# Attention by query tile: heads inside, Q, K and V kept on chip in F32, bias rows made between the attention's instructions

## The chip, the cores and the metric

The kernel runs on one core of a Trainium2 chip. The metric is device time in microseconds, from one launch to its end; lower is better. Shown are the median of the runs and, for the profile, one execution taken by the hardware profiler.

## The reference

The program computes attention with a learned position bias, then a mixture of experts, then a gated feed-forward block. Only the attention is touched here:

```python
B, H, S, D = (2, 8, 576, 64)              # hidden 32
scores = scale * np.matmul(q, k.transpose(0, 1, 3, 2))
psi_rel = np.log1p(np.abs(rel))           # rel = i - j
psi_i = np.log1p(np.maximum(pos[:, None].astype(np.float32), 1.0))
x = (psi_rel / psi_i)[..., None]
h = np.maximum(x @ w1 + b1, 0.0)
bias = h @ w2                             # [S, S, H], the same for both batches
scores = scores + bias.transpose(2, 0, 1)[None, :, :, :]
scores = scores - np.max(scores, axis=-1, keepdims=True)
attn = np.exp(scores)
attn = attn / (np.sum(attn, axis=-1, keepdims=True) + 1e-09)
return np.matmul(attn, v).astype(np.float32)
```

The output, 1152 rows of 512, goes to an expert gate (8 logits a row, the largest decides), to the chosen expert, and to the last block.

## The kernel before

**Engines and order.** TensorE (PE) multiplies, VectorE (DVE), ScalarE (ACT) and GpSimd (POOL) work on tiles, SyncE (SP) issues the DMAs. The order on each engine is the order of the program text (`manual_schedule`); every engine takes its instructions strictly in turn and waits on semaphores.

**Bias phase** (`bias_phase`, lines 478 to 583). A group `m` covers 16 query rows. `relus` makes four ReLU tiles of 128 x 576 from a table of logarithms: three on DVE (line 539), one on ACT (line 542). Eight matmuls (line 547), in four column tiles of 32, multiply them by w2, which gives 16 rows for 8 heads. `evict` copies the 128 x 576 sum out of PSUM (ACT, line 554) and writes it to a table in DRAM (line 558). All 36 groups come before the attention. Between them the first head's Q and K are split.

**Loads** (`loader`, lines 226 to 260). For each head and batch a tile with Q and K twice over is read (line 241). It is split into a high part in F32R and the rest: by ACT and DVE for the first head, by POOL (lines 252 to 257) for the others, one head ahead.

**Attention** (`attn_phase`, lines 263 to 475). Heads are outside; within a head come nine units (batch, query tile of 128 rows; the fifth tile has 64 rows of each batch and is one unit). For unit `u` the program issues: the score of `u + 1` (line 304, four F32R matmuls of 288 columns, eight for the fifth tile); the exponential of `u - 1` on ACT with row sums (line 336); the bound of `u` on DVE (line 319: scores times -1/8 plus bias and the row minimum in one instruction; line 209 to 214 load the bias rows of a head from the table); four transposes of `u - 2` (line 344) and a copy of the 128 x 512 result by ACT or DVE (lines 350, 352); tail transposes (line 360, copied in lines 362, 364). In pieces between units: P·V for half a head (line 378, F32, V as four column tiles of 32, 256 or 320 query columns), its copy (line 384) and `folds` (line 397), which adds the gate weights to the output columns, divides by the row sums (lines 408 to 417), writes the head's columns of all rows to DRAM (line 419) and adds the gate logits up in `lg` (line 423).

**After it** `route` turns `lg` into lists of rows for each expert, and `moe` gathers the rows from DRAM and runs experts and feed-forward. Both begin with the last sum in `lg`.

The PSUM buffers of attention and bias share tags: "S" (scores and bias sums), "T" (transposes), "P" (P·V).

Of the kernel before, what the change touches and what calls it, by code (L numbers as in the profile page):

```python
# [20 lines left out]
NQ = 5  # L21
SK = 640
SQ = 640
# [31 lines left out]
LOADS = (0, 3)  # L55
SHARE = 0.7
ON_A = (0, 2, 4, 6)
CUTS = (1, 3)
# [12 lines left out]
ND = 3  # L71
# [36 lines left out]
def pack(inputs):  # L108
    q, k, v = inputs["q"], inputs["k"], inputs["v"]
    qk = np.zeros((B, H, 128, SQ + SK), np.float32)  # L110
    qt, kt = q.transpose(0, 1, 3, 2), k.transpose(0, 1, 3, 2)
    for r in (slice(0, 64), slice(64, 128)):
        qk[:, :, r, :512] = qt[..., :512]
        for b in range(B):
            qk[b, :, r, 512 + b * 64:576 + b * 64] = qt[b, :, :, 512:]
        qk[:, :, r, SQ:SQ + 64] = kt[..., 512:]
        qk[:, :, r, SQ + 64:] = kt
    vt = np.zeros((H, 128, B, 6, D), np.float32)
    for t in range(4):
        vt[:, :, :, t] = v[:, :, t * 128:(t + 1) * 128].transpose(1, 2, 0, 3)  # L120
    for r in range(2):
        vt[:, r * 64:r * 64 + 64, :, 4 + r] = v[:, :, 512:].transpose(1, 2, 0, 3)
# [4 lines left out]
    fold = np.zeros((128, H // 2, RW + E), np.float32)  # L127
    for r in range(2):
        fold[r * 64:r * 64 + 64, :, E:RW] = np.eye(D)[:, None]
        fold[r * 64:r * 64 + 64, :, :E] = wg[::2].transpose(1, 0, 2)  # L130
        fold[r * 64:r * 64 + 64, :, RW:] = wg[1::2].transpose(1, 0, 2)
    both = np.zeros((128, H, B, RW), np.float32)
    for h in range(H):
        for r in range(2):
            both[r * 64:r * 64 + 64, h, r] = fold[r * 64:r * 64 + 64, h // 2, h % 2 * E:h % 2 * E + RW]
    a = {
        "qk": qk,
        "v": vt,
        "both": both,
        "wb": np.tile(wb, (4, 1)),  # L140
        "fold": fold,
        "ew1": inputs["moe_w1"],
        "ew2": inputs["moe_w2"],

        "mwg": inputs["moe2_w_gate"].view(np.int64),
        "mwv": inputs["moe2_w_val"].view(np.int64),
        "mwo": inputs["moe2_w_out"].view(np.int64),
    }
    a.update(constants())
    return {n: np.ascontiguousarray(x) for n, x in a.items()}  # L150
# [8 lines left out]
def build(tc, ins, out, cap):  # L159
    nc = tc.nc  # L160
    cap = max(0, min(int(cap), N))
    with ExitStack() as ctx:
# [19 lines left out]
        with ExitStack() as pctx:  # L182
            ps = pctx.enter_context(tc.tile_pool(name="ps", bufs=2, space=PSUM))
            attention(tc, ins, cst, rt, lg, x_p, rows, out, ps)
# [3 lines left out]
def attention(tc, ins, cst, rt, lg, x_p, rows, out, ps):  # L188
    nc = tc.nc
    with ExitStack() as ctx:  # L190
# [6 lines left out]
        nc.vector.memset(zi, 0.0)
        b_p = ctx.enter_context(tc.tile_pool(name="ab", bufs=2))
        heads = {}

        def bias_of(h, t):

            if h not in heads:
                heads[h] = b_p.tile([128, NQ, S], F32, name="bias")
            to = heads[h][:, t]
            src = table[t].rearrange("(q h) j -> q h j", h=H)[:, h]
            if t == 4:
                for r in (slice(0, 64), slice(64, 128)):
                    nc.sync.dma_start(to[r], src)
            elif t % 2:  # L210
                nc.sync.dma_start(to[:, 64:], src[:, :512])
                nc.sync.dma_start(to[:, :64], src[:, 512:])
            else:
                nc.sync.dma_start(to, src)

        load, qk = loader(tc, ctx, ins), {}
        ctx.enter_context(tc.manual_schedule(engines=ENGINES))
        with ExitStack() as bctx:
            loads = bias_phase(tc, bctx, ins, cst, rt, table, bias_of, zi, ps, load, qk)
        nc.sync.dma_start(fold, ins["fold"])  # L220
        nc.sync.dma_start(both, ins["both"])
        with ExitStack() as actx:
            attn_phase(tc, actx, (load, qk, loads), cst, (heads, bias_of), (fold, both), lg, x_p, rows, zi, out, ps)


def loader(tc, ctx, ins):

    nc = tc.nc
    raw_p = ctx.enter_context(tc.tile_pool(name="araw", bufs=4))
    qk_p = ctx.enter_context(tc.tile_pool(name="aqk", bufs=4))  # L230
    v_p = ctx.enter_context(tc.tile_pool(name="av", bufs=3))
    V, A, P = nc.vector, nc.scalar, nc.gpsimd
    one = ctx.enter_context(tc.tile_pool(name="az", bufs=1))
    zero = one.tile([128, 1], F32, name="zero")
    V.memset(zero, 0.0)
    vs = {}

    def load(h, b, hi="P"):

        raw = raw_p.tile([128, SQ + SK], F32, name="raw")  # L240
        nc.sync.dma_start(raw, ins["qk"][b, h])
        if h not in vs:
            vs[h] = v_p.tile([128, B, 6, D], F32, name="vt")
            nc.sync.dma_start(vs[h], ins["v"][h])
        QK = qk_p.tile([128, SQ + SK], F32R, name="QK")
        K2 = qk_p.tile([128, SK], F32R, name="K2")
        yield QK[:, :SQ], QK[:, SQ:], K2, vs[h]
        for o, n in ((0, SQ), (SQ, SK)):
            if hi == "A":
                A.activation(QK[:, o:o + n], raw[:, o:o + n], AF.Copy)  # L250
            else:
                P.tensor_tensor(QK[:, o:o + n], raw[:, o:o + n], view(zero, 0, (0, n)), op=ALU.add)  # L252
            yield
        low = V if hi == "A" else P
        low.tensor_tensor(QK[64:, :SQ], raw[64:, :SQ], QK[64:, :SQ].bitcast(F32), op=ALU.subtract)
        yield
        low.tensor_tensor(K2, raw[:, SQ:], QK[:, SQ:].bitcast(F32), op=ALU.subtract)
        yield

    return load  # L260


def attn_phase(tc, ctx, load, cst, bias, fold, lg, x_p, rows, zi, out, ps):
    nc = tc.nc
    V, A = nc.vector, nc.scalar
    s_p = ctx.enter_context(tc.tile_pool(name="as", bufs=3))
    one = ctx.enter_context(tc.tile_pool(name="apt", bufs=1))
    fold, both = fold
    pts = [one.tile([128, 4, B, S], F32, name=f"pt{n}") for n in range(2)]
    tls = [one.tile([128, B, 320], F32, name=f"tl{n}") for n in range(2)]  # L270
    os = [one.tile([128, 512], F32, name=f"o{n}") for n in range(2)]
    o8s = [one.tile([128, 128], F32, name=f"o8{n}") for n in range(2)]
    for n in range(2):
        nc.gpsimd.memset(tls[n][64:, :, 256:], 0.0)
        nc.gpsimd.memset(o8s[n][:64, 64:], 0.0)
        nc.gpsimd.memset(o8s[n][64:, :64], 0.0)
    m_p = ctx.enter_context(tc.tile_pool(name="am", bufs=4))
    ident = cst[:, C_ID:C_ID + 128]
    load, qk, loads = load
    heads, bias_of = bias  # L280
    seq = []
    for h in range(H):
        seq += [(h, b, t) for b in range(B) for t in (0, 1)] + [(h, -1, 4)]
        seq += [(h, b, t) for b in range(B) for t in (2, 3)]
    mid = {}
    spare = ps.tile([128, 512], F32, name="tt", bufs=1)
    sco, ex, sums, xhs = {}, {}, {}, {}

    def batches(u):
        h, b, t = seq[u]  # L290
        return (b,) if t < 4 else (0, 1)

    def score(u):

        h, b, t = seq[u]
        sc = ps.tile([128, 2, 512], F32, name="sc", tag="S")
        lhs = []
        for bb in batches(u):
            Q, K1, K2, _ = qk[h, bb]
            lhs += [(Q[:, t * 128:(t + 1) * 128], K) for K in (K1, K2)]  # L300
        o = 0 if t % 2 else 64
        for c in range(2):
            for n, (l, K) in enumerate(lhs):
                nc.tensor.matmul(  # L304
                    sc[:, c, :288], l, K[:, o + c * 288:o + (c + 1) * 288], start=n == 0, stop=n == len(lhs) - 1
                )
        sco[u] = sc

    def bound(u):
        h, b, t = seq[u]  # L310
        sc = sco.pop(u)

        if t % 2 == 0:
            pair = s_p.tile([128, 2, S], F32, name="ex")
            ex[u], ex[u + 1] = pair[:, 0], pair[:, 1]
            mid[u] = pair.rearrange("p a b -> p (a b)")[:, 512:640]
        e = ex[u]
        mx = m_p.tile([128, 1], F32, name="mx")
        V.tensor_tensor_reduce(  # L319
            e.rearrange("p (c j) -> p c j", c=2),  # L320
            sc[:, :, :288],
            heads[h][:, t].rearrange("p (c j) -> p c j", c=2),
            scale=-0.125,
            scalar=3.0e38,
            op0=ALU.add,
            op1=ALU.min,
            accum_out=mx,
        )
# [1379 lines left out]
```

## Time and profile before

| | us |
|---|---|
| median of 3 runs | 458.8 |
| lowest, highest | 455.86, 459.73 |
| the profiled execution | 455.44 |
| its span, first to last instruction | 453.7 |
| DVE's first ReLU of the bias phase | 5.26 |
| first bound of the attention | 64.82 |
| last bound of the attention | 222.07 |
| last sum of the gate logits (0.23 long) | 233.33 |

The busy time of an engine counts the time in which at least one of its instructions was under way. For PE this includes the latency of a pipelined matmul, which its neighbours overlap. A matmul on F32 tiles appears as two instructions, one on F32R tiles as one. "Idle before" is the engine's wait just before an instruction, with what ended it. PEclk is the granted share of TensorE's full clock.

### The profile page before, as it was taken

The numbers are of one execution on the slowest core, as the hardware profiler recorded it, in microseconds if no ns is written. First come the engines' busy times: TensorE is split into PE (matmuls) and PEld (weight loads), VectorE is DVE, ScalarE is ACT, GpSimd is POOL, SyncE is SP. The second block draws the span as 40 slices with busy tenths as digits, with TensorE's granted clock in tenths as the row PEclk, the third lists the DMA queues.
The fourth block names the chain that finished last, engine by engine and source line by source line (L and its number), as shares of the span: only waits on it lengthen the run. The fifth ranks groups of instructions, "written<-read, shape, count | busy, mean of one in ns | idle before, by whom it ended". The sixth has DMA issues, their size and how long they took to land. (4 is left out here: it accounts for less than half of the span.)

```text
span 453.7 us, 9220 instructions
## 1 busy us (share of the span) xinstructions
PE 409.4 (90%) x3493; PEld 321.9 (71%) x3493; DVE 310.3 (68%) x653; ACT 236.3 (52%) x459; POOL 100.3 (22%) x89
## 2 busy tenths in 40 slices
PE   8999897998998899899848789999999999999993
PEld 5333356766766676666635789898799999999982
DVE  6999974556657566655557458785488888888441
ACT  5999876555555564546422238563335554433321
POOL 0500009827283837540003210000000000000012
PEclk9999998999999999999976589999999999999999
DMA  7557868827466373910147993859105644440002
GB/s 258 211 195 225 308 248 271 280 71 262 134 198 209 122 251 91 318 56 1 51 122 242 345 309 95 277 181 331 48 1 170 209 175 143 141 140 1 1 25 93
DMA packets 53766, 77.22 MB, mean 170 GB/s; under 512 B 15090, under 2 KB 34162, under 8 KB 53712
## 3 DMA queue, kind: packets, MB, share of 16 engines
q1 hardware_dynamic: 52912, 74.05, 49.5%
q0 software_dynamic: 800, 2.48, 1.6%
q8 instruction: 30, 0.49, 0.5%
q14 instruction: 24, 0.20, 0.1%
HBM read 59.95 MB, written 16.58 MB: 169 GB/s over the span
## 5 line engine op out<-in xcount | busy, mean ns | idle before, releaser
L319 DVE CUSTOM_DVE_ANT_0 ex<-sc,bias 128x576 f32<-128x576 f32 x72 | 53.5, 752 | 22.8 <-issue 10.5
L1133 PE MATMUL pg<-x2l,swh 128*128 128x256 f32 (+1 forms) x192 | 58.1, 302 | 0.0
L1133 PE MATMUL pg<-x2h,swh 128*128 128x256 f32 (+1 forms) x192 | 58.0, 302 | 0.0
L1133 PE MATMUL pg<-x2h,swl 128*128 128x256 f32 (+1 forms) x192 | 57.9, 302 | 0.0
L336 ACT ACTIVATE ex<-ex,mx 128x576 f32<-128x576 f32 x72 | 55.4, 770 | 4.0 <-DVE mx L319 2.8
L304 PE MATMUL sc<-QK 128*128 128x288 f32 x160 | 52.0, 342 | 6.0 <-DVE mx L319 5.7
L547 PE MATMUL pb<-r,w 128*32 128x288 f32 x576 | 54.8, 415 | 2.6 <-ACT e L554 1.0
L539 DVE TENSOR_SCALAR r<-ltab,slope,neg 128x576 f32<-128x576 f32 x108 | 53.5, 570 | 0.1
L352 DVE COPY pt<-tp 128x512 f32<-128x512 f32 x40 | 27.6, 690 | 31.9 <-PE tp L344 31.8
L547 PEld LDWEIGHTS pb<-r,w 128*32 128x32 f32 x576 | 21.6, 108 | 35.3 <-DVE r L539 13.4
L304 PE MATMUL sc<-K,QK 128*128 128x288 f32 x160 | 45.3, 299 | 0.0
L304 PEld LDWEIGHTS sc<-QK 128*128 128x128 f32 x160 | 30.5, 191 | 20.6 <-issue 10.8
L344 PE MATMUL tp<-cst,ex 128*128 128x128 f32 x288 | 43.9, 276 | 0.3 <-ACT ex L336 0.3
L252 POOL TENSOR_TENSOR QK<-raw,zero 128x640 fp32r<-128x640 f32 x28 | 34.5, 1253 | 33.4 <-DMA raw<-in_qk 18.6
L1140 ACT ACTIVATE wh<-wr 128x608 fp32r<-128x608 f32 (+2 forms) x13 | 8.8, 674 | 61.8 <-DVE wr L1136 61.8
L350 ACT ACTIVATE pt<-tp 128x512 f32<-128x512 f32 x32 | 19.1, 597 | 40.0 <-PE tp L344 39.1
L1158 POOL DMA_INDIRECT out<-xr,ids x2 | 2.0, 1012 | 170.7 <-DMA xr<-rows,ri 170.7
L1133 PEld LDWEIGHTS pg<-x2h,swh 128*128 128x128 f32 x192 | 36.2, 189 | 2.0 <-issue 0.8
L1133 PEld LDWEIGHTS pg<-x2l,swh 128*128 128x128 f32 x192 | 36.1, 188 | 0.9
L344 PEld LDWEIGHTS tp<-cst,ex 128*128 128x128 f32 x288 | 35.8, 142 | 1.2 <-ACT ex L336 0.8
L1133 PEld LDWEIGHTS pg<-x2h,swl 128*128 128x128 f32 x192 | 36.2, 188 | 0.0
L378 PE MATMUL po<-pt,vt 128*32 128x320 f32 (+1 forms) x512 | 35.8, 410 | 0.1
(191 smaller groups left out, 894.8 us busy)
## 6 DMA issues: line engine op xcount, KB each, us to landing
wr<-in_ew SPq DMA_DIRECT2D x24, 512.0 KB, 4.9
table<-e SPq DMA_DIRECT2D x36, 288.0 KB, 2.1
raw<-in_qk SPq DMA_DIRECT2D x16, 640.0 KB, 6.1
w<-in_mwg SPq DMA_DIRECT2D x12, 512.0 KB, 3.6
w<-in_mwv SPq DMA_DIRECT2D x12, 512.0 KB, 4.7
w<-in_mwo SPq DMA_DIRECT2D x12, 512.0 KB, 6.7
bias<-table SPq DMA_DIRECT2D x16, 288.0 KB, 6.3
bias<-table SPq DMA_DIRECT2D x16, 256.0 KB, 6.1
```

Of the source, the lines that this page charges most:

```text
L252: P.tensor_tensor(QK[:, o:o + n], raw[:, o:o + n], view(zero, 0, (0, n)), op=ALU.add)
L304: nc.tensor.matmul(sc[:, c, :288], l, K[:, o + c * 288:o + (c + 1) * 288], start=n == 0, stop=n == len(lhs) - 1)
L319: V.tensor_tensor_reduce(e.rearrange("p (c j) -> p c j", c=2), sc[:, :, :288], heads[h][:, t].rearrange("p (c j) -> p c j", c=2), scale=-0 ...
L336: A.activation(ex[u], ex[u], AF.Exp, bias=mx, scale=-1.0, accum_out=sums[h][:, col:col + 1])
L344: nc.tensor.transpose(x[:, kt], e[:, kt * 128:(kt + 1) * 128], ident)
L350: A.activation(to, x, AF.Copy)
L352: V.tensor_copy(to, x)
L378: nc.tensor.matmul(po[s * 32:s * 32 + 32, c:c + m], v[:, s // 2, kt, s % 2 * 32:s % 2 * 32 + 32], x[:, s // 2], start=k == 0, stop=k == 4, ...
L539: V.tensor_scalar(r, x, slope[:, g:g + 1], neg, op0=ALU.mult, op1=ALU.max)
L547: nc.tensor.matmul(pb[s * 32:s * 32 + 32, c, :half], w2, rs[s][:, c * half:(c + 1) * half], start=True, stop=True, tile_position=(0, s * 32),)
L1133: nc.tensor.matmul(pg, w[:, a * 4 + kk], x[:, kk, cs], start=kk == 0 and i == 0, stop=kk == 3 and i == 2)
L1140: A.activation(sh[:, cs], sg[:, cs], AF.Copy)
```

## The change

Query tiles are now outside and heads inside: 40 pairs (head, tile), each with both batches at once. The bias rows of a query tile serve all heads of that tile, so only the groups of the first tile and three more (`alone`, 11 groups) are made ahead; the other 25 are made one in each iteration of the attention loop, with the fourth ReLU on POOL instead of ACT, and the product in two halves with an eviction each. K and Q of both batches lie one above the other in 64 rows each, V as it is, all in F32, loaded once and kept. A score is one matmul of 128 columns for the last 64 keys of both batches and two of 512 columns that use 64 rows of the array each (`tile_position=(b * 64, 0)`). P·V, fold and scaling are done for each pair, over 128 query columns. The rows of a tile are written to DRAM after its last head, and the gate logits of a tile are summed over heads by one reduction there.

The core of the diff:

```diff
+PAIRS = [(h, t) for t in range(NQ) for h in range(H)]
...
+    def relus(self, m, alone):
...
+            r = self.r_p.tile([128, S], F32, name=f"r{s}")
+            if s < ND or not alone:
+                (nc.vector if s < ND else nc.gpsimd).tensor_scalar(
+                    r, x, self.slope[:, g:g + 1], self.neg, op0=ALU.mult, op1=ALU.max
+                )
+            else:
+                nc.scalar.activation(r, x, AF.Relu, bias=self.b1, scale=self.slope[:, g:g + 1])
...
+    def evict(self, m, c, x, alone):
...
+        self.nc.scalar.activation(e, x, AF.Identity, bias=self.off[:, 0 if alone else 1:][:, :1])
+        if c != 0:
+            t, k = divmod(m, 8)
+            self.nc.sync.dma_start(self.table[t][k * 128:(k + 1) * 128], self.e.pop(m))
...
+        def bias_of(p):
+            h, t = PAIRS[p]
+            to = bt[p] = b_p.tile([128, S + 64], F32, name="bias")
...
+                nc.sync.dma_start(to[:, 64:], src)
                 nc.sync.dma_start(to[:, :64], src[:, 512:])
...
+        def score(p):
...
+            sc = sco[p] = ps.tile([128, 3 * 512], F32, name="sc", tag="S", bufs=1)
...
+            if t < 4:
+                nc.tensor.matmul(
+                    view(sc, 512, (448, 2), (1, 64)), Q, T.rearrange("p (b j) -> p b j", b=2), start=True, stop=True
+                )
+                for b in range(B):
+                    r = slice(b * 64, b * 64 + 64)
+                    nc.tensor.matmul(
+                        sc[:, b * 1024:b * 1024 + 512], Q[r], K[r], start=True, stop=True, tile_position=(b * 64, 0)
+                    )
             else:
...
+                nc.tensor.matmul(sc[:, :512], Q, K, start=True, stop=True)
+                for n in range(2):
+                    nc.tensor.matmul(sc[:, 512:576], Q, T[:, n * 64:n * 64 + 64], start=n == 0, stop=n == 1)
...
+        def product(p):
...
+            po = ps.tile([128, 512], F32, name="po", tag="P", bufs=1)
...
+        def fold(p):
...
+            f = outs[p] = ps.tile([128, 512], F32, name="pf", tag="P", bufs=1)
...
+        alone = 8 + AHEAD
+        bias.offsets()
+        last = None
+        for m in range(alone):
+            bias.relus(m, True)
+            late = bias.whole(m)
+            if last:
+                last()
...
+                if m == 8:
+                    for p in range(3):
+                        bias_of(p)
+            last = late
+        score(0)
+        last()
+        bias.relus(alone, False)
...
+        for p in range(np_ + 2):
+            g = alone + p
+            g = g if g < S // 16 else None
+            live = p < np_
+            if g is not None:
+                x = ps.tile([128, 512], F32, name="pb", tag="pb", bufs=1)[:, :S // 2]
+                bias.product(g, 0, x)
+                bias.evict(g, 0, x, False)
+            if live:
+                for b in range(nb(p)):
+                    mx[b] = bound(p, b)
+                expo(p, 0, mx[0])
+            if p >= 2:
+                product(p - 2)
+            if g is not None:
+                x = ps.tile([128, 512], F32, name="pb", tag="pb", bufs=1)[:, :S // 2]
+                bias.product(g, 1, x)
+            if live and nb(p) == 2:
+                expo(p, 1, mx[1])
+            if g is not None:
+                bias.evict(g, 1, x, False)
+                if g + 1 < S // 16:
+                    bias.relus(g + 1, False)
+            if 1 <= p <= np_:
+                turn(p - 1)
+            if p >= 2:
+                fold(p - 2)
+            if p + 1 < np_:
+                score(p + 1)
+            if 1 <= p <= np_:
+                turned(p - 1, "A")
+                turned(p - 1, "V")
+                inverse(p - 1)
+            if p >= 2:
+                scaled(p - 2)
+            if p + 3 < np_:
+                bias_of(p + 3)
+            for x in todo.get(p, ()):
+                load(x)
+            if 16 <= p < 19:
+                P.tensor_copy(*raw[p - 16])
```

## Rows read from the trace of the kernel before

**Rows 1.** The profile's head: the span.
```profile
span 453.7 us, 9220 instructions
```

**Rows 2.** Windows: attention loop, drain, routing; busy us of each engine, granted clock, DMA.
```profile
63.70:222.07 158.37, 141.41 (x1452) 108.56 (x1455) 96.42 (x257) 87.44 (x225) 80.86 (x69) 0.99 0.53 168
222.07:233.60 11.53, 8.04 (x116) 5.24 (x108) 4.86 (x17) 2.89 (x9) 0.00 (x0) 1.00 0.17 49
233.60:255.10 21.50, 13.49 (x112) 9.63 (x112) 15.08 (x67) 6.01 (x11) 5.49 (x6) 0.58 0.85 271
```

**Rows 3.** Groups by form, bias phase: shapes, count, busy us, mean ns, idle before.
```profile
L547 PE MATMUL pb<-r,w 128*32 128x288 f32 x576 | 54.8, 415 | 2.6 <-ACT e L554 1.0 <-ACT r L542 0.8
L539 DVE TENSOR_SCALAR r<-ltab,slope,neg 128x576 f32<-128x576 f32 x108 | 53.5, 570 | 0.1
L554 ACT ACTIVATE e<-pb,off 128x576 f32<-128x576 f32 x36 | 26.6, 738 | 4.7 <-PE pb L547 2.4 <-DMA table<-e 1.5 <-ACT e L554 0.7
```

**Rows 4.** Groups by form, attention loop.
```profile
L336 ACT ACTIVATE ex<-ex,mx 128x576 f32<-128x576 f32 x72 | 55.4, 770 | 4.0 <-DVE mx L319 2.8
L319 DVE CUSTOM_DVE_ANT_0 ex<-sc,bias 128x576 f32<-128x576 f32 x72 | 53.5, 752 | 22.8 <-issue 10.5 <-PE sc L304 6.3 <-ACT e L554 2.9
L344 PE MATMUL tp<-cst,ex 128*128 128x128 f32 x288 | 43.9, 276 | 0.3 <-ACT ex L336 0.3
L352 DVE COPY pt<-tp 128x512 f32<-128x512 f32 x40 | 27.6, 690 | 31.9 <-PE tp L344 31.8
L378 PE MATMUL po<-pt,vt 128*32 128x320 f32 x256 | 20.3, 438 | 0.0
L350 ACT ACTIVATE pt<-tp 128x512 f32<-128x512 f32 x32 | 19.1, 597 | 40.0 <-PE tp L344 39.1 <-DMA table<-e 1.0
L252 POOL TENSOR_TENSOR QK<-raw,zero 128x640 fp32r<-128x640 f32 x28 | 34.5, 1253 | 33.4 <-DMA raw<-in_qk 18.6 <-PE tp L344 13.1 <-PE tt L360 1.6
L378 PE MATMUL po<-tl,vt 128*32 128x128 f32 x243 | 9.9, 279 | 0.0
L362 ACT ACTIVATE tl<-tt 128x128 f32<-128x128 f32 x32 | 8.7, 272 | 4.6 <-PE tt L360 4.4
L410 DVE TENSOR_TENSOR xh<-tt,rs 128x288 f32<-128x288 f32 x15 | 6.9, 458 | 7.4 <-PE tt L402 5.6 <-DVE rs L409 1.2 <-DMA vt<-in_v 0.2
L409 DVE RECIPROCAL rs<-rs 128x4 f32<-128x4 f32 x15 | 2.7, 181 | 0.5
```

**Rows 5.** Timeline of PE at 131.6 us: start us, length, instructions merged.
```profile
131.58 0.48 PE L378 MATMUL po<-pt,vt 128*32 128x320 f32 x4
...
131.58 1.28 PE L378 MATMUL po<-pt,vt 128*32 128x320 f32 x16
132.79 0.40 PE L304 MATMUL sc<-QK 128*128 128x288 f32 x1
```

**Rows 6.** Timeline of POOL's casts and a DVE ReLU beside one.
```profile
13.23 5.60 POOL L526 CAST mask<-maskf 128x256 bf16<-128x256 f32 x1 [12.77 <-DMA maskf<-in_mask]
...
19.54 0.77 DVE L539 TENSOR_SCALAR r<-ltab,slope,neg 128x576 f32<-128x576 f32 x1
19.57 0.43 POOL L526 CAST iota<-iotaf 128x288 f16<-128x288 f32 x1
```

**Rows 7.** Timeline of DVE's first ReLUs and first bound; DMA issues before 70 us.
```profile
5.26 13.31 DVE L539 TENSOR_SCALAR r<-ltab,slope,neg 128x576 f32<-128x576 f32 x27
...
64.82 0.76 DVE L319 CUSTOM_DVE_ANT_0 ex<-sc,bias 128x576 f32<-128x576 f32 x1 [2.88 <-ACT e L554]
...
table<-e SPq DMA_DIRECT2D x36, 288.0 KB, 2.1
...
bias<-table SPq DMA_DIRECT2D x2, 288.0 KB, 3.0
```

**Rows 8.** Timeline of DVE: the last bound and the last sum of the logits.
```profile
222.07 0.75 DVE L319 CUSTOM_DVE_ANT_0 ex<-sc,bias 128x576 f32<-128x576 f32 x1
...
233.33 0.23 DVE L423 TENSOR_TENSOR lg<-lg,xh 128x72 f32<-128x72 f32 x1
```

More of the change, by code (lines that the diff above doesn't have):

```diff
@@ L21 @@
 NQ = 5
-SK = 640
-SQ = 640
+KQ1, KQ2 = 768, 512
 NT = 9
@@ L125, in pack @@
     wg = inputs["moe_w_gate"].reshape(H, D, E)
[L127 to L131, printed above, removed]
     both = np.zeros((128, H, B, RW), np.float32)
[L133 to L135 removed]
+    for b in range(B):
+        r = slice(b * 64, b * 64 + 64)
+        both[r, :, b, :E] = wg.transpose(1, 0, 2)
+        both[r, :, b, E:] = np.eye(D)[:, None]
     a = {
[L137 to L138 removed]
+        "kq1": kq[:, :, :KQ1],
+        "kq2": kq[:, :, KQ1:],
+        "vm": vm,
+        "vt": vt,
         "both": both,
         "wb": np.tile(wb, (4, 1)),
[L141 removed]
         "ew1": inputs["moe_w1"],
@@ L189, in attention @@
+def attention(tc, ins, cst, rt, lg, rows, out, ps):
     nc = tc.nc
+    V, A, P = nc.vector, nc.scalar, nc.gpsimd
     with ExitStack() as ctx:
@@ L193, in attention @@
         table = [dram.tile([(128 if t < 4 else 64) * H, S], F32, name=f"table{t}") for t in range(NQ)]
-        fold = one.tile([128, H // 2, RW + E], F32, name="fold")
+        kq1 = [one.tile([128, KQ1], F32, name=f"kq1{h}") for h in range(H)]
+        kq2 = [one.tile([128, KQ2], F32, name=f"kq2{h}") for h in range(H)]
+        vm = [one.tile([128, B, 4, D], F32, name=f"vm{h}") for h in range(H)]
+        vt = one.tile([128, H, 3, D], F32, name="vt")
         both = one.tile([128, H, B, RW], F32, name="both")
@@ L196, in attention @@
         zi = one.tile([128, DM], F32, name="zi")
[L197 to L205, printed above, removed]
+        tl4 = [one.tile([128, 128], F32, name=f"tl4{n}") for n in range(2)]
+        o4 = [one.tile([128, 128], F32, name=f"o4{n}") for n in range(2)]
+        raw = [(rt[n], one.tile(list(rt[n].shape), F32, name=n + "f")) for n in ("mask", "ids", "iota")]
@@ L218, in attention @@
[L218 to L250, printed above, removed]
-            else:
[L252 to L260, printed above, removed]
@@ new lines, in nb, with bound @@
+        def nb(p):
+            return B if PAIRS[p][1] < 4 else 1
+        def bound(p, b):
+            if b == 0:
+                pairs[p] = e_p.tile([128, B, S], F32, name="ex")
+                sums[p] = m_p.tile([128, B], F32, name="sum")
+            mx = m_p.tile([128, 1], F32, name=f"mx{b}")
+            o = 0 if b else 64
+            V.tensor_tensor_reduce(
+                pairs[p][:, b], sco[p][:, 960:] if b else sco[p][:, :S], bt[p][:, o:o + S],
+                scale=-0.125, scalar=3.0e38, op0=ALU.add, op1=ALU.min, accum_out=mx,
+            )
+            return mx
@@ new lines, in fold, with inverse @@
+        def fold(p):
+            h, t = PAIRS[p]
+            o, w = outs.pop(p), both[:, h]
+            f = outs[p] = ps.tile([128, 512], F32, name="pf", tag="P", bufs=1)
+            if t < 4:
+                nc.tensor.matmul(f[:, :B * RW], o, w.rearrange("p b c -> p (b c)"), start=True, stop=True)
+            else:
+                for b in range(B):
+                    nc.tensor.matmul(f[:, :RW], o, w[:, b], start=b == 0, stop=b == 1)
+        def inverse(p):
+            n = nb(p)
+            V.tensor_scalar(sums[p][:, :n], sums[p][:, :n], 1e-9, None, op0=ALU.add)
+            V.reciprocal(sums[p][:, :n], sums[p][:, :n])
@@ new lines, in scaled @@
+        def scaled(p):
+            h, t = PAIRS[p]
+            n = nb(p)
+            if h == 0:
+                xs[t] = x_p.tile([128, B, H, RW], F32, name="x")
+            x = xs[t]
+            V.tensor_tensor(
+                x[:, :n, h], outs.pop(p)[:, :n * RW].rearrange("p (b c) -> p b c", b=n),
+                view(sums.pop(p), 0, (1, n), (0, RW)), op=ALU.mult,
+            )
+            if h == H - 1:
+                to = view(lg, t * E, (4 * E, n), (1, E)) if t < 4 else lg[:, 8:]
+                V.tensor_reduce(to, view(x, 0, (H * RW, n), (1, E), (RW, H)), axis=AX.X, op=ALU.add)
+                for b in range(n):
+                    r = (b * 4 + t if t < 4 else 8) * 128
+                    nc.sync.dma_start(rows[r:r + 128].rearrange("p (h d) -> p h d", h=H), x[:, b, :, E:])
@@ new lines, in attention @@
+        todo = {n: [] for n in range(-36, 40)}
+        for n, x in ((2, 2), (9, 3)):
+            todo[n - 36].append(("kq1", x))
+        todo[5 - 36].append(("vm", 1))
+        for p in range(4):
+            todo[p].append(("kq1", p + 4))
+        for p in range(6):
+            todo[p].append(("vm", p + 2))
+        for h in range(H):
+            todo[h + 3].append(("kq2", h))
+        for n in range(3):
+            todo[12 + n].append(("raw", n))
+        for n in range(NT):
+            todo[14 + 2 * n].append(("out", n))
@@ new lines, in attention @@
+        for x in (("kq1", 0), ("kq1", 1), ("vt", 0), ("both", 0), ("vm", 0)):
+            load(x)
+        warm = ps.tile([128, 512], F32, name="warm", tag="tt", bufs=1)
+        for n in range(WARM0):
+            nc.tensor.matmul(warm[:, :256], zi[:, :128], zi[:, :256], start=True, stop=True)
+        early = one.tile([1, 1], F32, name="early")
+        A.activation(early, zi[:1, :1], AF.Exp)
+        alone = 8 + AHEAD
[6 more added lines that the diff above has]
+                last()
+                for x in todo[m - 1 - 36]:
+                    load(x)
+                if m == 8:
+                    for p in range(3):
+                        bias_of(p)
+            last = late
```

487 lines of the change are left out of this document (166 added, 321 removed).

## Prediction

> **What bounds the kernel now.** I read the page's head first, then busy time by stage, then the groups of instructions by form, then the timeline at the seams. The profiled execution took 455.44 us and its span is 453.7 us [rows 1]. TensorE counts as busy for 141.4 of the 158.4 us of the attention loop, 89% [rows 2]. That is not 89% of peak: matmuls are pipelined, so each row carries a latency that overlaps its neighbours. Two rows of one line give the true rate: the P·V matmul takes 438 ns with 320 columns and 279 ns with 128 [rows 4], so an instruction takes (438 - 279) / 192 = 0.83 ns per column, and some 0.17 us is latency. A matmul in F32 stands in the trace as two instructions (line 378 writes 256 matmuls over 256 or 320 columns, and 512 are recorded), so it occupies the array for 1.66 ns per column. The timeline confirms it: two steps of 320 columns, four column tiles each, 16 instructions, start at 131.58 and the next matmul starts at 132.79; 1.21 us = 4 x 0.266 + 0.15 [rows 5]. It also shows that the four column tiles run together: four instructions of 0.438 us are over in 0.48 us [rows 5].
>
> Four stages follow from the windows and the seams. The bias phase runs from 5.26 to 63.7, with the first bound at 64.82 [rows 7], and is VectorE's: 27 ReLUs in 13.31 us is 0.493 each, three to a group of 16 rows, so 1.48 us a group and 36 groups [rows 3, 7]. The attention loop runs from there to the last score bound at 222.07; beside PE's 141.4 us DVE is busy 96.4, ACT 87.4 and POOL 80.9 [rows 2]. No engine is full; PE waits 11% of the loop. Then the pipeline drains until the gate logits are summed at 233.56 (233.33 + 0.23) [rows 8]. Routing and the MoE follow, 220.1 us to the end of the span, and hang on those logits alone.
>
> **The change part by part.** The diff leaves routing and the MoE as they are, so I compute when the logits are ready and add 220.1 us. PE's granted clock is 0.58 between 233.6 and 255.1 [rows 2], the stretch after the drain; the new kernel drains in the same way, so I take that stretch as it is (a price of 2 us either way stays in the range).
>
> *Start.* 11 groups stand alone instead of 36. ReLUs start at 5.26 as before; the new loads come behind the same first five transfers. The ReLUs for group 8 end at 5.26 + 9 x 1.48 = 18.6, the eviction of group 7 behind them takes 0.74 [rows 3], its write lands 2.1 us after issue and a bias read 3.0 us after its own [rows 7]. The reads wait on the SP queue for that write; with 0.8 us allowed for the issues the first bias tile is there at 18.6 + 0.74 + 2.1 + 3.0 + 0.8 = 25.2. DVE has by then made the ReLUs of group 11 (5.26 + 12 x 1.48 = 23.0), so the first bound starts at 25.2, not at 64.8.
>
> *Scores.* The two F32R products of split halves go. In their place stand one F32 matmul of 128 columns for both batches' tails (0.21 us) and two of 512 columns, K of 64 rows, in two row tiles. One of them is 512 x 1.66 = 0.85 us. The trace of before has no row tile; from both sides: 0.85 for the two if they run together as the column tiles do, 1.70 if one after the other. I take 0.85, because the column tiles are the nearest row.
> The Trainium skill, "TensorEngine Tiling (Array Packing)", Key Properties, says that tiles work independently of each other, and that a change of tiling mode drains the array. The trace agrees on the first for column tiles, with 0.48 us for four; no run so far shows row tiles. By that rule the sum would be the one below.
> A change between column tiles and the whole array costs 0.15 here (1.21 - 1.06 [rows 5]); three changes in a pair are 0.45.
>
> *One iteration, a pair (head, tile) with both batches, on PE:* bias products 2 x 288 columns 0.96; P·V five steps of 128 columns 1.06; nine transposes at 276 - 170 = 0.106 [rows 4], 0.96; the fold, 144 columns, 0.24; scores 0.21 + 0.85; changes 0.45. Sum 4.73 us.
> *On DVE:* two bounds with their accumulator reads 1.52, three ReLUs 1.48, one copy 0.69, reciprocal and its addition 0.35, the scaling 0.35 (144 columns against 0.458 for 288) [rows 3, 4]. Sum 4.39 us.
> *On ACT:* two exponentials 1.54, the eviction in two halves 0.74 to 1.48, one copy 0.60, two small copies under 0.60 each [rows 3, 4]: 3.4 to 4.8 us, never the longest.
> In order on PE: bias product, P·V, bias product, transposes, fold, next score. The waits inside: P·V needs the shared bank "P" from the scaling two heads back, DVE's last work of the iteration before, covered by the 0.48 us of bias product ahead of it. The fold needs ACT's copy of P·V, which stands behind the first exponential: 0.2 + 0.75 + 0.1 + 0.77 + 0.27 = 2.1 us [rows 4] after the score, and the transposes end at 3.1, so it is covered. The next score needs both bounds read (1.7 us after the last score), also covered. DVE's copy waits for the transposes (3.2), just when its ReLUs end (0.2 + 1.52 + 1.48). So the order closes at 4.73 without a stall, but DVE is 93% full. Bounds: 4.73, and 4.73 x 1.12 = 5.3 with the 11% that PE waits in the loop of before. I take 5.1.
> 25 such iterations; 7 more without a bias group, 3.77 to 4.2, taken 4.0.
> *The fifth tile,* 8 iterations of one bound each, is a chain instead: score to bound 0.2 + 0.83, exponential 0.1 + 0.77, two copies behind it on ACT 0.5, fold 0.15 + 0.25, next score 1.07: 3.9 us, taken 3.95. These lose: the 71 units from 64.82 to 222.07 took 2.21 us each, and a fifth tile was one unit.
> *Drain.* From the last bound: 0.83 + exponential 0.9 + five transposes 0.8 + copies 0.9 + P·V 0.8 + copies 0.6 + fold 0.4 + scaling and reduction over heads 0.9: 6.2 us, where 222.07 to 233.56 is 11.5 [rows 8].
> The first two iterations have no copy, fold or scaling and are about 2.5 us shorter together.
>
> Sum: 25.2 + 25 x 5.1 - 2.5 + 7 x 4.0 + 7 x 3.95 + 6.2 = 212.1, against 233.6: 21.5 us less, 455.4 - 21.5 = 433.9 for the profiled execution. The runs shown lie 0.4 to 4.3 us above that execution (median 458.8), so I add 2: **436 us**.
>
> *Costed at nothing.* The hi/lo splits, nearly all of POOL's 80.9 us [rows 2], ran beside the loop; what they leave is one ReLU per iteration, taken from ACT, near 1.25 us by the 640-column row [rows 4], with over 5 us until its matmul. The splits of the first head stand inside the bias phase and go with it. Q, K and V are read once, half the bytes; those reads were hidden. The bias reads are three iterations (15 us) ahead of their use; at a tile's first head SP waits for the last table write, 2.1 us, and behind it stand only later loads and table writes. If that cover went, each tile's first bound would be late by 5 us, 20 us in all.
>
> **The rivals.**
> (a) The row tiles do not overlap. 0.85 more in each of 32 iterations, on the engine that sets the pace: 27 us, 463 us, slower. It decides from 21.5 / 32 = 0.67 us more a pair, a pair of row tiles above 1.5 us. For it: each F32 matmul is two instructions, and only column tiles are seen to run together. Half an overlap (three beats of 0.43) gives 14 us, 450.
> (b) VectorE becomes the bound through GpSimd's ReLU. While DVE ran ReLUs back to back, a POOL cast of 256 elements took 5.60 us, one of 288 elements 0.43, and a DVE ReLU beside the latter took 0.77 instead of 0.57 [rows 6]: the two do hinder each other. Bounds: 0.2 a pair (4.6, still under PE: nothing) and a whole POOL operation, 1.25 (5.64 plus waits: 14 to 20 us, 450 to 456). Against the high end: in the loop before, POOL was busy half the time and the bound kept 752 ns [rows 2, 4], and the ReLUs at 13 to 18 us kept their pace beside the long cast [rows 6, 7]. I take the low end.
> The Trainium skill, "GPSIMD Engine Reference", Specifications, says that GpSimd shares its SBUF interfaces with VectorE, with contention where a VectorE instruction runs in a two-port mode or has two SBUF inputs. The trace agrees with 5.60 against 0.43 us. The rule sets no price, so it moves neither bound.
> (c) The loop closes without waits: T = 4.73 and 3.8 give 10 us less, 426.
>
> **How the numbers follow.** Forecast (428 to 444): 0.60. Half an overlap or (b) high, 444 to 455: 0.20. Rival (a) in full, or several late buffers at once, above 455: 0.13. Rival (c), below 428: 0.07. The range 426 to 455 leaves out the third and half of the last. One per cent, 4.6 us, is what a measurement here can tell from no change: faster by more (under 454.2) 0.82; within 0.09; slower 0.09, nearly all of it (a).
>
> **What would show it.** The first bound near 25 us; iterations of 5 us between bounds of one batch, then 4; the two score matmuls of 512 columns starting within 0.1 us of each other (right) or 0.43 or more apart (a); DVE ReLUs at 0.57 us (right) or near 1 (b); logits near 212 us and 220 us from there. The forecast is wrong if iterations pass 5.7 us, or if the stretch behind the logits changes by more than 3 us.

## The result and the profile after

| | before | after |
|---|---|---|
| median of the runs, us | 458.25 (455.86 to 459.73) | 438.11 (436.6 to 440.72) |
| profiled execution, us | 455.44 | 438.22 |
| span of it, us | 453.7 | 436.4 |
| ratio after / before | | 0.957, interval 0.951 to 0.963 |

The change takes off 20.1 us in the medians and 17.3 in the two spans; the profiled execution of before is the lowest of its four runs, that of after lies at its median. Each ratio below is against runs of the kernel before on the same chip. The kernel before has medians of 458.25, 458.81 and 457.17 us in its three sets of runs, so a difference of 1 or 2 us between two kernels of different sets shows nothing by itself.

Window of after from the first bound to the last (columns as in [rows 2]), and VectorE's last sum of the gate logits, which ends at 216.50:

```profile
27.82:208.22 180.40, 171.65 (x2516) 116.87 (x2520) 127.57 (x363) 110.19 (x310) 61.59 (x27) 0.98 0.58 174
...
216.23 0.27 DVE L451 TENSOR_REDUCE lg<-x 128x8 f32<-128x64 f32 x1
```

The first bound moved from 64.82 [rows 7] to 27.82: 37.0 us less. From there to the logits it takes 188.7 us instead of 233.56 - 64.82 = 168.7: 20 us more. The difference is the gain of 17. TensorE is now busy for 171.65 of 180.40 us, 95% where it was 89% [rows 2]. Behind the logits there remain 436.4 - 216.50 = 219.9 us (before: 220.1).

The groups by form of after for the ReLUs, VectorE's as in [rows 3] (count, busy us, mean ns, idle before):

```profile
L230 DVE TENSOR_SCALAR r<-ltab,slope,neg 128x576 f32<-128x576 f32 x108 | 55.3, 577 | 1.6 <-PE pw L239 1.4 <-PE px L239 0.2
L230 POOL TENSOR_SCALAR r<-ltab,slope,neg 128x576 f32<-128x576 f32 x25 | 64.7, 2589 | 74.5 <-PE pb L239 51.5 <-DVE r L230 20.4 <-PE tp L379 2.6
```

VectorE's ReLU kept its length (577 ns, 570 before). GpSimd's ReLU took 2.59 us, twice the 1.25 that the prediction put near it.

Timeline of PE over one iteration that makes a bias group (start us, length, instructions merged; the second row of line 344 is from a narrower window and shows the first two of the four instructions):

```profile
104.39 0.69 PE L239 MATMUL pb<-r,w 128*32 128x288 f32 x8
104.90 1.06 PE L411 MATMUL po<-pt,vm 128*32 128x128 f32 x32
106.00 0.67 PE L239 MATMUL pb<-r,w 128*32 128x288 f32 x8
106.59 1.09 PE L379 MATMUL tp<-cst,ex 128*128 128x128 f32 x8
107.63 0.41 PE L427 MATMUL pf<-both,o 128*128 128x144 f32 x2
107.88 0.38 PE L339 MATMUL sc<-kq,kq 128*128 128x128 f32 x2
108.19 1.13 PE L344 MATMUL sc<-kq,kq 64*128 64x512 f32 x4
...
108.19 0.70 PE L344 MATMUL sc<-kq,kq 64*128 64x512 f32 x2
...
109.25 0.69 PE L239 MATMUL pb<-r,w 128*32 128x288 f32 x8
```

No row names a wait: TensorE goes from product to product, 109.25 - 104.39 = 4.86 us a turn. Read off the starts: bias products 0.51 and 0.59, P·V with the keys' tail 1.10, transposes with theirs 1.04, fold 0.25, score tail 0.31, the two matmuls of 512 columns 1.06. These are four instructions, over in 1.13 us, and the first two of them are over in 0.70; two run at a time, so the two row tiles run together.

Timeline of VectorE in after, bounds of one batch in consecutive pairs: with a bias group, without one, and of the fifth tile:

```profile
104.51 0.76 DVE L361 CUSTOM_DVE_ANT_0 ex<-sc,bias 128x576 f32<-128x576 f32 x1 [0.41 <-PE sc L344]
109.37 0.76 DVE L361 CUSTOM_DVE_ANT_0 ex<-sc,bias 128x576 f32<-128x576 f32 x1 [0.41 <-PE sc L344]
...
157.00 0.76 DVE L361 CUSTOM_DVE_ANT_0 ex<-sc,bias 128x576 f32<-128x576 f32 x1
160.89 0.76 DVE L361 CUSTOM_DVE_ANT_0 ex<-sc,bias 128x576 f32<-128x576 f32 x1 [0.41 <-PE sc L344]
...
191.91 0.76 DVE L361 CUSTOM_DVE_ANT_0 ex<-sc,bias 128x576 f32<-128x576 f32 x1 [1.06 <-PE sc L350]
195.99 0.76 DVE L361 CUSTOM_DVE_ANT_0 ex<-sc,bias 128x576 f32<-128x576 f32 x1 [1.07 <-PE sc L350]
```

4.86, 3.89 and 4.08 us. In the first case VectorE stands 0.41 us for the score, so PE sets the pace and not VectorE. In the last it stands 1.07 us: a chain through all engines, as the prediction had it. The experiment on the fifth tile's copies tests this.

Two places lost time. The second is the drain, which comes with the experiment on the fifth tile. The first is the start; timeline of after from the first bias reads on:

```profile
24.48 0.32 SPq L329 DMA_DIRECT2D bias<-table  x1
27.23 1.65 SPq L253 DMA_DIRECT2D table<-e  x2
27.82 0.76 DVE L361 CUSTOM_DVE_ANT_0 ex<-sc,bias 128x576 f32<-128x576 f32 x1 [3.19 <-DMA bias<-table]
31.67 0.50 ACT L250 ACTIVATE e<-pb,off 128x288 f32<-128x288 f32 x1 [5.83 <-DMA table<-e]
32.23 1.19 PE L239 MATMUL pb<-r,w 128*32 128x288 f32 x8 [4.86 <-ACT e L250]
34.07 2.08 PE L344 MATMUL sc<-kq 64*128 64x512 f32 x4
36.20 0.76 DVE L361 CUSTOM_DVE_ANT_0 ex<-sc,bias 128x576 f32<-128x576 f32 x1 [4.73 <-PE sc L344]
```

The bias reads wait on SP for the last write of the first query tile's table, until 24.48; the table writes of groups 8 and 9 stand behind them and go out only at 27.23. The eviction of group 11 needs a buffer of "e" (the tile that holds the evicted bias rows) that one of these writes still holds, and waits 5.83 us. On ACT the first exponential stands behind that eviction, and on PE the second half of the bias product. So the second pair's bound comes at 36.20, 8.38 us after the first. The score at 34.07 takes 2.08 us instead of 1.13.

### The profile page after: what moved, and what is told of

It is laid out like the page before. It is cut to its first block, busy times and chain, and to the rows that moved or that the text cites. A ratio compares the mean times of both kernels' runs of the same rounds, so it can differ in the third digit from the quotient of the medians.

```text
span 436.4 us, 10658 instructions
## 1 busy us (share of the span) xinstructions
PE 400.6 (92%) x4205; PEld 314.9 (72%) x4205; DVE 300.3 (69%) x675; ACT 223.1 (51%) x501; POOL 80.7 (18%) x53
## 5 line engine op out<-in xcount | busy, mean ns | idle before, releaser
L230 POOL TENSOR_SCALAR r<-ltab,slope,neg 128x576 f32<-128x576 f32 x25 | 64.7, 2589 | 74.5 <-PE pb L239 51.5
L250 ACT ACTIVATE e<-pb,off 128x288 f32<-128x288 f32 x50 | 24.9, 497 | 46.7 <-PE pb L239 34.3
L411 PEld LDWEIGHTS po<-pt,vm 128*32 128x32 f32 x1280 | 32.4, 110 | 12.1 <-ACT tl L393 6.4
L379 PEld LDWEIGHTS tp<-cst,ex 128*128 128x128 f32 x288 | 30.8, 141 | 13.6 <-issue 12.9
L239 PE MATMUL pb<-r,w 128*32 128x288 f32 x400 | 35.1, 423 | 5.6 <-ACT e L250 5.6
L411 PE MATMUL po<-pt,vm 128*32 128x128 f32 (+1 forms) x1280 | 39.3, 263 | 0.8 <-DVE sum L435 0.4
L1087 PEld LDWEIGHTS pg<-x2h,swh 128*128 128x128 f32 x192 | 36.2, 189 | 2.0 <-issue 0.8
L1087 PEld LDWEIGHTS pg<-x2h,swl 128*128 128x128 f32 x192 | 36.2, 188 | 0.0
L395 DVE COPY pt<-tp 128x512 f32<-128x512 f32 x32 | 22.1, 692 | 18.2 <-PE tt L383 9.8
L1090 DVE TENSOR_TENSOR wr<-pg,wr 128x256 f32<-128x256 f32 (+1 forms) x48 | 21.7, 471 | 16.3 <-PE pg L1087 12.2
L239 PEld LDWEIGHTS pb<-r,w 128*32 128x32 f32 x400 | 9.8, 110 | 27.1 <-ACT tl L393 17.4
L909 DVE TENSOR_TENSOR swl<-wf,swh 128x512 fp32r<-128x512 f32 x36 | 23.8, 688 | 5.4 <-ACT swh L908 5.3
```

Of the source, the lines that this page charges most:

```text
L230: (nc.vector if s < ND else nc.gpsimd).tensor_scalar(r, x, self.slope[:, g:g + 1], self.neg, op0=ALU.mult, op1=ALU.max)
L239: self.nc.tensor.matmul(to[s * 32:s * 32 + 32], self.w2, self.rs[m][s][:, c * (S // 2):(c + 1) * (S // 2)], start=True, stop=True, tile_po ...
L250: self.nc.scalar.activation(e, x, AF.Identity, bias=self.off[:, 0 if alone else 1:][:, :1])
L379: nc.tensor.transpose(y[:, k], x[:, b * 640 + k * 128:b * 640 + (k + 1) * 128], ident)
L395: V.tensor_copy(pts[p][:, 1], tps[p][1])
L411: nc.tensor.matmul(po[s * 32:s * 32 + 32, :w], v, x, start=k == 0, stop=k == 4, tile_position=(0, s * 32),)
```

## The experiments

All seven start from the kernel after.

**Six buffers for the finished bias rows.**

```diff
-        self.e_p = ctx.enter_context(tc.tile_pool(name="bie", bufs=3))
+        self.e_p = ctx.enter_context(tc.tile_pool(name="bie", bufs=6))
```

> The changed kernel with six buffers instead of three for the evicted bias tile, nothing else. Theory 1: the 8.4 us of the first iteration come from the SP queue: the table writes of groups 8 and 9 stand behind bias reads that wait for the write of group 7, their tiles stay occupied, ACT's eviction of group 11 waits 5.8 us for one, and behind it stand the first exponential and, on PE, the second score. With free tiles the eviction follows its product at 27.4, the second pair's first bound comes near 32 instead of 36.2, and the whole is 4 to 5 us shorter, 433 to 434 us. Rival: that eviction only hides the first bias read, which lands at 27.8 and 29.2 anyway, and the halved PE clock; then the second pair starts no earlier than 35 and the whole moves by less than 1.5 us.

433.39 us (431.15 to 435.29), ratio to before 0.946 (0.941 to 0.952). Timeline of this kernel, the eviction of group 11 and the first two bounds:

```profile
25.91 0.50 ACT L250 ACTIVATE e<-pb,off 128x288 f32<-128x288 f32 x1 [1.72 <-PE pb L239]
26.51 0.76 DVE L361 CUSTOM_DVE_ANT_0 ex<-sc,bias 128x576 f32<-128x576 f32 x1 [3.45 <-DMA bias<-table]
29.93 0.74 DVE L361 CUSTOM_DVE_ANT_0 ex<-sc,bias 128x576 f32<-128x576 f32 x1
```

The eviction now waits for its product only, and the second pair follows the first by 3.42 us instead of 8.38. With nothing else changed, this shows the buffers to be the cause: 4.7 us in the medians, 5.0 between these rows.

**Both matmuls of 512 columns in one row tile.**

```diff
-                    r = slice(b * 64, b * 64 + 64)
+                    r = slice(0, 64)
...
-                        sc[:, b * 1024:b * 1024 + 512], Q[r], K[r], start=True, stop=True, tile_position=(b * 64, 0)
+                        sc[:, b * 1024:b * 1024 + 512], Q[r], K[r], start=True, stop=True, tile_position=(0, 0)
```

> Both score matmuls of 512 columns use the first batch's 64 rows of the array (so the second batch's scores are computed from the first batch's Q and K); number, sizes and order of all instructions stay. Theory: two row tiles run together and one row tile cannot, so each of the first 32 iterations gets longer by one matmul, 0.85 us: 5.7 us instead of 4.86, 4.74 instead of 3.89, 27 us in all, 465 us. Rival: PE has room in the iteration (the loop is held by the chain through DVE and ACT), then less than half of it, under 13 us, shows.

467.92 us (467.76 to 468.08), ratio 1.020 (1.013 to 1.028). Timeline of PE and VectorE in this kernel:

```profile
106.49 1.98 PE L344 MATMUL sc<-kq,kq 64*128 64x512 f32 x4
...
102.80 0.76 DVE L361 CUSTOM_DVE_ANT_0 ex<-sc,bias 128x576 f32<-128x576 f32 x1 [1.25 <-PE sc L344]
108.51 0.76 DVE L361 CUSTOM_DVE_ANT_0 ex<-sc,bias 128x576 f32<-128x576 f32 x1 [1.25 <-PE sc L344]
```

The four instructions take 1.98 us, 0.85 more than in two row tiles, and the iteration 5.71, 0.85 more as well. So rival (a) had the right size: 32 x 0.85 = 27 us, 30 measured. Some of the excess lies at the start, where in this execution the granted clock of TensorE stood at half until 43.9 us instead of 37.7. Without the overlap of the row tiles the rest of the change is slower than the kernel before, by 1.3 to 2.8%.

**The fourth ReLU on VectorE instead of GpSimd.**

```diff
-                (nc.vector if s < ND else nc.gpsimd).tensor_scalar(
+                nc.vector.tensor_scalar(
```

> The fourth ReLU of the 25 interleaved groups on DVE instead of POOL. Theory: POOL's ReLU (2.59 us) costs DVE nothing, and DVE, which is idle for 0.4 us of an iteration, gets 0.52 us more: an iteration goes from 4.86 to about 5.0, the whole 2 to 5 us longer, 440 to 443 us. Rival (contention): POOL slows DVE's own ReLUs and copies in the loop; without it they get faster, and an iteration stays at 4.86 or falls.

440.41 us (437.72 to 443.45), ratio 0.963 (0.956 to 0.969). Windows over eight iterations, the kernel after first, then this one:

```profile
104.51:143.39 38.88, 38.88 (x588) 26.33 (x590) 32.83 (x89) 25.81 (x72) 21.71 (x12) 1.00 0.58 175
```

```profile
104.50:143.38 38.88, 38.88 (x587) 26.32 (x585) 36.09 (x98) 25.80 (x73) 0.43 (x1) 1.00 0.57 175
```

The longer iteration that was expected did not come: eight of them take 38.88 us either way. VectorE took over the work, 36.09 us busy instead of 32.83, and still had room. Its ReLU takes 575 ns here and 577 with GpSimd beside it. So neither VectorE nor a contention with GpSimd sets the pace; GpSimd's help in the steady loop was worth nothing. The medians' difference of 2.3 us is inside the spread of these runs. In the profiled execution the second iteration alone is longer, 6.65 us instead of 4.97, with TensorE's granted clock at half until 41.4 us instead of 37.7; whether the fourth ReLU on VectorE has a part in that is not shown.

**All 36 bias groups ahead of the loop.** What is left of the change is the new score without the splits, the new pairs and the new drain.

```diff
-AHEAD = 3
+AHEAD = 28
...
-        bias.relus(alone, False)
```

> All 36 bias groups ahead of the attention, none in the loop; pairs, row tiles and F32 as in the changed kernel. Theory: interleaving is the gain. 25 groups more ahead cost 25 x 1.47 = 36.8 us; the first 25 iterations fall from 4.86 to 3.89, 24.3 us; the 5 us lost in the first iteration go, as all table writes are issued long before: 445 to 447 us, some 8 us longer than the changed kernel. Rival: the gain lies in the new loop (pairs, scores in row tiles) and the interleaving only moves work: within 3 us of the changed kernel.

450.52 us (450.01 to 451.92), ratio 0.983 (0.977 to 0.989). Timeline of VectorE in this kernel, the first bound:

```profile
68.66 0.76 DVE L361 CUSTOM_DVE_ANT_0 ex<-sc,bias 128x576 f32<-128x576 f32 x1 [3.21 <-PE sc L344]
```

The first bound is 68.66 - 27.82 = 40.8 us later, and the 25 iterations take 3.89 us (110.97 to 114.86), 0.97 less each, 24.3 in all; the two first iterations come without their stall. The expectation was some 4 us too low: the phase at the start became longer than that of before, 68.66 against 64.82. Of the change's 20.1 us, the bias rows made inside the loop are worth 450.5 - 438.1 = 12.4, and all the rest about 8: 8.3 against this set's median of before, 458.81, and 7.7 against the 458.25 above. The parts of this rest were not separated. The 12.4 are what the stall at the start leaves, since this kernel does not have it; against the kernel with six buffers, 433.39, the interleaving is worth 17.1.

**The fifth tile's small copies on VectorE.** In the kernel after, ACT runs them between the next pair's exponential and its copy of the transposes. The timeline of after at the last pairs:

```profile
209.03 0.78 ACT L369 ACTIVATE ex<-ex,mx 128x576 f32<-128x576 f32 x1 [2.08 <-DVE mx L361]
209.80 0.45 ACT L420 ACTIVATE o<-po 64x64 f32<-64x64 f32 x2
210.30 0.67 PE L430 MATMUL pf<-both,o 128*128 128x72 f32 x4 [0.72 <-ACT o L420]
211.00 0.23 DVE L445 TENSOR_TENSOR x<-pf,sum 128x72 f32<-128x72 f32 x1 [1.75 <-PE pf L430]
211.38 0.65 PE L411 MATMUL po<-pt,vm 128*32 128x64 f32 x32 [0.42 <-DVE sum L435]
212.08 0.66 PE L379 MATMUL tp<-cst,ex 128*128 128x128 f32 x4
```

The last exponential is over at 209.81, but its transposes start at 212.08: on PE they stand behind the P·V of the pair before. That P·V starts at 211.38, released by VectorE: its bank "P" is free only when the fold of the pair before it has been scaled (211.00 to 211.23). This fold waits for the small copies "o", and on ACT they stand behind the last exponential. The trace puts the wait down to line 435, VectorE's instruction beside that scaling; that the scaling is what frees the bank follows from the program.

```diff
-                    A.activation(o[r, r], po[r, :w], AF.Copy)
+                    V.tensor_copy(o[r, r], po[r, :w])
```

> The changed kernel with the two 64x64 copies of P.V of the fifth tile's pairs on DVE instead of ACT, nothing else. Theory: an iteration of the fifth tile (4.08 us) is the chain score, bound, exponential, these copies, fold, next score; on DVE the copies stand behind the bound and not behind the exponential, so the chain loses the exponential, 0.8 us: 3.3 us an iteration, 5 to 6 us in all, and about 0.5 more in the drain: 432 to 433 us. Rival: these iterations are held by something else (P.V behind the scaling of the pair before, or the transposes), then they stay above 3.8 us and the whole above 436 us.

433.64 us (432.91 to 434.9), ratio 0.950 (0.947 to 0.954). Timeline of this kernel in the fifth tile:

```profile
197.11 0.76 DVE L361 CUSTOM_DVE_ANT_0 ex<-sc,bias 128x576 f32<-128x576 f32 x1 [1.06 <-PE sc L350]
197.84 0.46 DVE L420 COPY o<-po 64x64 f32<-64x64 f32 x2
197.91 0.78 ACT L369 ACTIVATE ex<-ex,mx 128x576 f32<-128x576 f32 x1 [1.80 <-DVE mx L361]
200.41 0.76 DVE L361 CUSTOM_DVE_ANT_0 ex<-sc,bias 128x576 f32<-128x576 f32 x1 [1.06 <-PE sc L350]
```

The copies run beside the exponential, not behind it, and the iteration takes 3.30 us instead of 4.08. The logits are ready 5.3 us earlier, at 211.2. The rival, that something else holds these iterations above 3.8 us, is out.

**The bias reads behind the table writes.** This asks whether the order on SP's queue is what held the buffers. The three reads are issued after the writes of groups 8 to 10; the buffers stay at three.

```diff
-                if m == 8:
-                    for p in range(3):
-                        bias_of(p)
             last = late
...
         last()
+        for p in range(3):
+            bias_of(p)
```

> The changed kernel, three buffers for the evicted bias tile as in it, but the first three pairs' bias reads are issued on the SP queue behind the table writes of groups 8 to 10 instead of before them. Theory: the place on the SP queue is the cause and the buffers only carry it. The writes no longer wait for the write of group 7, so ACT's eviction of group 11 comes at its product, near 27.5; the reads are issued 1.5 to 2 us later, so the first bound comes near 29.5 instead of 27.8, the second pair's near 33 instead of 36.2: 3 us shorter, 435 us. Rival: three buffers are too few in either order, ACT waits some 4 us again, and nothing is won: 438 us or more.

438.0 us (437.19 to 438.71), ratio 0.959 (0.956 to 0.963). Timeline of this kernel:

```profile
26.40 0.37 SPq L329 DMA_DIRECT2D bias<-table  x1
27.68 0.50 ACT L250 ACTIVATE e<-pb,off 128x288 f32<-128x288 f32 x1 [1.72 <-PE pb L239]
31.23 0.76 DVE L361 CUSTOM_DVE_ANT_0 ex<-sc,bias 128x576 f32<-128x576 f32 x1 [6.46 <-DMA bias<-table]
35.29 0.76 DVE L361 CUSTOM_DVE_ANT_0 ex<-sc,bias 128x576 f32<-128x576 f32 x1 [1.15 <-PE sc L344]
```

The eviction of group 11 waits for its product alone, so the order, with only three buffers, was the cause. But the expected gain did not come: the reads go out at 26.40 instead of 24.48, the first bound starts 3.4 us later, and only 0.9 us is left at the second pair. Here whichever goes first on the queue delays the other, and with 438.0 us nothing is won, as the rival had it, though not by its reason; with six buffers the writes can wait.

**Three together:** six buffers, the copies on VectorE, and ACT's copy of the offsets behind its first ReLU. That copy waits for eight small matmuls, which stand on PE behind its warm-up matmuls, and in the kernel after ACT starts its first ReLU only behind it, at 7.85 us; VectorE then stands for ACT's part of the first groups.

```diff
-        bias.offsets()
...
             bias.relus(m, True)
+            if m == 0:
+                bias.offsets()
```

> Three edits together: six buffers for the evicted bias tile, the fifth tile's copies on DVE, and the eight matmuls and the copy of the bias offsets behind the first group's ReLUs, so that ACT's first ReLU does not wait 2.8 us for them. Theory: the three places do not touch; 4.7 us, 5.5 us and about 1 us: 427 us, faster than both kernels. Rival: what is won at the start is lost again where the first bias read waits for its table, and the last edit brings nothing: 428.5 us or more.

427.32 us (426.71 to 428.4, five runs), ratio 0.936 (0.933 to 0.939). Its timeline at both ends of the attention:

```profile
4.70 0.87 ACT L234 ACTIVATE r<-ltab,wb,slope 128x576 f32<-128x576 f32 x1 [2.47 <-DMA ltab<-in_ltab]
26.00 0.76 DVE L361 CUSTOM_DVE_ANT_0 ex<-sc,bias 128x576 f32<-128x576 f32 x1 [3.31 <-DMA bias<-table]
204.49 0.27 DVE L451 TENSOR_REDUCE lg<-x 128x8 f32<-128x64 f32 x1
```

ACT's first ReLU starts at 4.70, the logits are ready at 204.76 (204.49 + 0.27), 11.7 us before those of the kernel after. This version is faster than both kernels, by 10.8 and 29.9 us in the medians (each from its own runs). The first bound comes only 0.5 us before that of the six buffers alone and still waits 3.31 us for its bias rows, so the earlier ReLUs gave little there.

## Why the prediction was right, and where its terms were off

Faster was right, and 438.1 us lies 2 from the 436 forecast. That it is so near is in part luck. The terms of the sum failed in opposite directions, the iteration by -5.4 us and the first two iterations by +5.7. And the sum itself, 433.9 for the profiled execution, was 4.3 short of the 438.22 measured; the 2 us added because the profiled execution of before lay below its median hide half of that, since the one of after lies at its own.

| term of the sum | predicted, us | measured, us | difference |
|---|---|---|---|
| first bound | 25.2 | 27.82 | +2.6 |
| first two iterations | 2 x 5.1 - 2.5 = 7.7 | 8.38 + 4.97 = 13.35 | +5.7 |
| 23 more with a bias group | 23 x 5.1 = 117.3 | 111.94 | -5.4 |
| 7 without | 28.0 | 27.18 | -0.8 |
| 7 steps of the fifth tile | 27.65 | 27.93 | +0.3 |
| drain | 6.2 | 8.28 | +2.1 |
| logits ready | 212.1 | 216.50 | +4.4 |
| behind them | 220.1 | 219.9 | -0.2 |

**The iteration.** The sum of PE's products, 4.73, was 0.13 short of the 4.86 measured. A step that failed is the allowance: I took 5.1 because PE had waited 11% of the loop of before, and the new order leaves it no wait at all. For an order written out by hand, the waits of the old order say little of the new one; the check of each wait in the prediction (P·V, fold, next score: all covered) was the better evidence, and it pointed at 4.73. The 0.13 lie in what stands between the products: without the three changes the sum was 4.28, so these changes, with all that the sum left out, come to 0.58 where it had 0.45.

**The row tiles.** 0.85 us for the two was right up to the changes of mode around them, 1.06 from start to start, and the experiment with one row tile shows that without the overlap nothing of the gain is left. The Trainium skill, "TensorEngine Tiling (Array Packing)", Key Properties, has the tiles work independently. The trace agrees for row tiles, 1.13 us against 1.98. Rival (a) and its half are out.

**The start, the term that failed.** The prediction walked the SP queue and wrote that behind the waiting reads "stand only later loads and table writes". The table writes are the point: each holds a buffer of "e" until it has landed, ACT's next eviction waits for one of three, and the first exponential and the next bias product wait behind that eviction. I asked what stands behind the wait on the queue, not what those transfers still hold, and put them at nothing. Six buffers give 3.42 us instead of 8.38 to the second pair; the reads moved behind the writes show the same wait gone. In the first bound's +2.6, ACT's late first ReLU and a stall of VectorE take part: VectorE stands 1.40 us until 9.50 in the kernel after, and not in the version of three. How much each gives was not separated. With six buffers alone the bound came 1.3 us earlier, but not by the buffers alone: PE's warm-up matmuls, the same 14 in both, took 4.78 us in that execution and 6.00 in that of the kernel after, so ACT's first ReLU started at 6.63 instead of 7.85, and VectorE did not stand there.

Timeline of after, the rows of that stall:

```profile
7.85 1.63 ACT L234 ACTIVATE r<-ltab,wb,slope 128x576 f32<-128x576 f32 x2
9.50 2.05 DVE L230 TENSOR_SCALAR r<-ltab,slope,neg 128x576 f32<-128x576 f32 x4 [1.40 <-PE pw L239]
```

**The drain.** The prediction summed the last pair's own chain, 6.2 us, as if the pair before were done. It was not: the last transposes stand on PE behind that pair's P·V, until 212.08, 2.27 us after the last exponential is over, which accounts for the +2.1. With the copies on VectorE the drain took 7.5 us, 203.72 to 211.2, so part of it remains.

**VectorE and GpSimd.** Rival (b) took GpSimd's ReLU at 1.25 us and was off by two: 2.59. The mechanism it feared costs nothing in the loop: in the kernel after each ReLU of VectorE takes 572 to 584 ns, and GpSimd's 2.59 us are hidden by the iteration's 4.86. So the low end, which the prediction took, was right. That the two engines never hinder each other is not shown; the last section has a row that speaks against it.

**Rival (c)** came true for the loop: no waits, 4.86 and 3.89. Its 426 us are nearly reached (427.3) once the start and the fifth tile are mended too, but by another sum: the fifth tile's steps then take 3.30 us, where (c) kept 3.95.

## What to carry to other kernels

When work moves from a phase of its own into the steady loop, price the loop by the engine that sets its pace, product by product, and look for the losses at the seams: the first iteration and the drain. At a queue that waits, ask not only which transfers stand behind it but which buffers they hold, and which instruction on another engine needs one of these; three more buffers there gave 4.7 us. A helper engine's share is worth only what the helped engine lacks: here VectorE had room, and in the steady loop the help gave nothing.

## What the runs showed of the hardware beyond expectation

Two F32 matmuls of 64 rows and 512 columns in two row tiles take 1.13 us, in one row tile 1.98: the overlap is full, 0.85 us being the 512 x 1.66 ns of one.

GpSimd needs 2.59 us for an element-wise ReLU that takes VectorE 0.577, a factor of 4.5. Most of that is GpSimd's own pace: the one at 33.62 takes 2.28 us, and VectorE is idle all the while, from 31.5 to 36.2. In the loop, where GpSimd's begins beside VectorE's last ReLU, most take 2.63 us; that this ReLU is what slows them was not tested. Line 230 of after (shortest, median and longest in ns) and that row:

```profile
L230 POOL TENSOR_SCALAR r<-ltab,slope,neg x25: 2279/2633/2883, 23.7 to 140.9; 128x576 f32<-128x576 f32 x25
...
33.62 2.28 POOL L230 TENSOR_SCALAR r<-ltab,slope,neg 128x576 f32<-128x576 f32 x1 [4.71 <-PE pb L239]
```

VectorE's ReLU can be the longer one too. In the kernel with six buffers one that began while GpSimd's was under way took 1.06 us instead of 0.575, and ended 0.3 us after GpSimd's; the two before it, beside the same ReLU of GpSimd, took 0.67 and 0.57. What decides between them is not shown:

```profile
27.42 2.27 POOL L230 TENSOR_SCALAR r<-ltab,slope,neg 128x576 f32<-128x576 f32 x1
28.95 1.06 DVE L230 TENSOR_SCALAR r<-ltab,slope,neg 128x576 f32<-128x576 f32 x1
```

The wait at the start has a second price, in TensorE's clock. Windows of the kernel after, then of the one with six buffers (granted clock third from the right):

```profile
30.90:37.70 6.80, 5.04 (x22) 1.41 (x22) 2.07 (x7) 2.65 (x7) 2.28 (x1) 0.50 0.69 206
```

```profile
30.90:37.70 6.80, 6.33 (x89) 4.30 (x90) 5.78 (x15) 5.38 (x15) 3.46 (x2) 1.00 1.04 386
```

In the kernel after, TensorE was idle from 27.4 to 32.2 (4.86 us), and the clock stood at half, the lower of its two levels (1.2 and 2.4 GHz), from 30.9 to 37.7; it was granted in full from 27.3 to 30.9 and from 37.7 to 41.0: the bias product took 1.19 us instead of 0.69 and the score 2.08 instead of 1.13. With six buffers the gap is not there and the clock stays at its upper level.
